# Exp groups of two PSUM banks with a third shared bank up to group 600, 101 VectorE quads, and the reciprocal multiply on GpSimd, in a fused attention and gated MLP block

## Chip, cores and metric

The kernel runs on one core of a Trainium2 chip. The metric is the device time in microseconds (us) of one execution. A core has five engines that work side by side: TensorE (PE in the profile, PEld for its weight loads), VectorE (DVE), ScalarE (ACT), GpSimd (POOL) and SyncE (SP), which here issues nearly all DMA transfers. TensorE writes its results into PSUM, eight banks of 128 partitions x 512 fp32 values; the other operands lie in SBUF.

## What is computed

The input x has 2048 rows of 640 values. The reference is a transformer block with modulation (adaLN), all weights in bf16:

```python
mod = (_silu(c) @ w_mod).reshape(c.shape[0], 6, 1, -1)   # sa, ca, ga, sb, cb, gb
h = _layernorm(x) * (1 + ca) + sa
x = x + ga * A(h)      # attention: 32 heads of 20, softmax(q k^T / sqrt(20)) v, then @ wo
h = _layernorm(x) * (1 + cb) + sb
x = x + gb * B(h)      # B(h) = ((h @ w_gate) * (h @ w_up)) @ w_down, inner width 1536
```

The 32 x 2048 x 2048 softmax exponentials are the large elementwise part.

## The kernel before

**Tiling.** The queries are cut into five chunks of 512, 512, 512, 256 and 256 rows (CHUNKS, L400). The heads are taken four at a time, in 8 sets; a chunk with a set of heads is an item, so there are 40 items. Within an item the work is cut into units: one head, one PSUM bank of scores (128 keys x 512 queries, or 2 x 128 keys x 256 queries). An item of a 512-row chunk has 64 units, one of a 256-row chunk has 32. Scores stand with keys on the partitions. Score matmuls (L1204) use 32 rows of TensorE each, so four heads run side by side; the matmuls with V (L1666) use 32 columns each, so again four run side by side, all into PSUM bank 7.

**Two ways to an exponential.** Most units go to ScalarE: one ACTIVATE (L1238) takes a group of neighbouring score banks and writes bf16 probabilities into a ring (PPs, L547, 4 slots for each of two sets). The groups alternate between bank set A, which starts at bank 0, and set B, which starts at bank 3. Up to group HEADG (60, L404) every group has two banks; from then on set A has three banks (0, 1, 2) and set B two (3, 4); L1078 decides it. The other units go to VectorE, in quads of four units; QUADS (L401) says how many quads an item has. For a unit VectorE evacuates the scores as integers (L1262); for a quad it then makes a mantissa part (L1290), a product (L1295) and an exponent part (L1298), which stand for the exponential as a sum of two terms. Both terms are multiplied with V, so such a unit costs two V matmuls in place of one. D_LEAD sets how early within the sequence a quad's scores are due.

**PSUM.** Five banks belong to the exp groups and bank 7 to the V accumulation. The rest is the pool G (L619), from which everything else takes its bank: projections of Q, K and V, the output projection, the MLP, the VectorE quads' scores and filler matmuls. G starts with banks 5, 6 and 2. Bank 2 leaves it when group HEADG is near (HEAD_OUT groups ahead, L1817) and then serves as the third bank of set A.

**After an item.** When all V matmuls of an item are done, VectorE transposes the accumulator (L1343), takes the reciprocal of the softmax sums (L1346), multiplies (L1348) and transposes back (L1355); DMAs put the result in place for the output projection. With T3_POOL (L407) the multiply goes to GpSimd instead, on all items but the last (L1351).

**What sets the order.** A planner in the program (class Sched, L114) plays all tasks through at build time with costs of its own and writes a fixed instruction order for each engine, with semaphore waits. TensorE's turn is chosen in pick_pe (L1814): a score group first if its banks are free, with up to two units of VectorE quads attached to it; then V matmuls, then the other work by priority and gate (the number of exp groups started), then filler matmuls where TensorE's recent activity is low. Until STEAL_END (L25) ScalarE may take over PSUM evacuations from VectorE when it has nothing to do (steal, L240). After chunk c its output projection, second layernorm and MLP (suffix, L1388) run spread over the exps of chunk c + 1, by GATE_F; after the last chunk they form the tail. The K projections of a key tile in K_ALL go directly into place (kq_round, L878); those of the others are computed packed, five rounds of up to 128 columns, written to DRAM and read back in the layout that the scores need (packed_round, L929).

```python
1078        us = ubuf[ap:ap + (3 if even and len(glist) >= HEADG else 2)]
...
1817        if HEADG and g >= HEADG - HEAD_OUT and 2 not in G.gone:
1818            G.retire(2)
```

Of the kernel before, what the change touches and what calls it, by code (L numbers as in the profile page):

```python
# [6 lines left out]
ALU = mybir.AluOpType  # L7
# [14 lines left out]
T0 = 700.0  # L22
DMA_SLOW = 0.0015
DMA_LAT = 1700.0
STEAL_END = 94936.728  # L25
STEAL_GAP = 300.0
HAM_W = 3413.3
HAM_MIN = 2550.0
# [369 lines left out]


CHUNKS = [(0, 512), (512, 512), (1024, 512), (1536, 256), (1792, 256)]  # L400
QUADS = [(3, 3, 3, 3, 3, 3, 4, 3), 3, (3, 3, 3, 3, 3, 3, 4, 3), (1, 2, 1, 2, 1, 2, 0, 2), 1]  # L401
D_LEAD = 0.35
NB0, NSS = 2, 3
HEADG = 60  # L404
GU_ONE = 0
XCONT = 0
T3_POOL = 0  # L407
HEAD_OUT = 1
NPS = 4
TS_4X, TT_2X = 600.0, 1145.0  # L410
WM_GATE = 18
WM_NEED = 1.721
K_DIRECT = (0, 1, 2, 3)
Q_DIRECT = 2
K_LEAD = 0.567
K_ALL = (0, 1)
KD_LEAD = 0.559
DMA_WINDOW = 900000
D_LATE = 12
D_RES = 92  # L420
PVMIN, PVMAX, PVCAP = 2, 11, 18
GATE_F = [0.8, 0.893, 0.938, 0.5, 1.0]
FILL_MIN = 4200.0
DUP_MIN = 0.0
XN_POOL = ()
XFIRST = 0
LN2P = 1.495
NALT = 1
OPFIRST = 0
HT_L = 0.072  # L430
V_L = 0
LATE_A = 1.174
LATE_L = 2.164
LATEQ = (3,)
LATEQ_A = 7
LATEQ_F = 0.73
QUAD_GAIN = 0.597233983857778
NTERM = 2

# [9 lines left out]
def build_kernel(nc, A_x, A_wqkv, A_wo, B_x, B_w_gate, B_w_up, B_w_down, c, w_mod, out):  # L449
# [5 lines left out]
    NSET = 8  # L455
# [141 lines left out]

    set_r = (hprod, h2T, xck, xn2)
    ntail = CHUNKS[-2][1]
    q_dead = sum(NSET * n * 2 for (_, n) in CHUNKS[:-1])  # L600
    set_t = None
    t_size = 0
    if NALT:
        T = Sub(qt_off, sum(NSET * n * 2 for (_, n) in CHUNKS[:2]))
        set_t = (T.alloc("hprodt", [128, FT, ntail], BF16), T.alloc("h2Tt", [128, KD, ntail], BF16),
                 T.alloc("xckt", [128, ntail // 128, D], BF16), T.alloc("xn2t", [128, ntail // 128, D], BF16))
        t_size = T.off - qt_off
# [661 lines left out]
    for qi, (it, us) in enumerate(dquads):  # L1269
        st_ = d_state[qi]  # L1270
        st_["src"], st_["ss"] = {}, {}

        def term(f, deps, dur, name, slot=None, src=None, last=False, it=it, qi=qi, st_=st_):
            t = Task("dve", dur, f, deps, prio=2.5 + .001 * qi, name=f"{name}.{qi}")
            if slot is not None:
                t.acq = [(sSS, "s", 1)]
            t.cond = lambda: it <= st_pv["item"]

            def on_t(task):
                if slot is not None:  # L1280
# [12 lines left out]
        def fx(e, st_=st_):  # L1293
            d = DSS[:, st_["ss"][0], :].bitcast(BF16)
            return e.tensor_tensor(d, DB0[:, st_["slot"], :].bitcast(BF16), d, ALU.mult)  # L1295

        def fe(e, st_=st_):
            return e.tensor_scalar(DSS[:, st_["ss"][1], :], DB0[:, st_["slot"], :], 0x7F80, 2, op0=ALU.bitwise_and,  # L1298
                                   op1=ALU.bitwise_or)
        tm = term(fm, list(st_["p1"]), TS_4X, "M", slot=0)  # L1300
        term(fx, [tm], TT_2X, "X", src=0, last=True)
        term(fe, list(st_["p1"]), TS_4X, "EX", slot=1, src=1, last=True)

    first_pv = {}
# [276 lines left out]
    for it in range(len(items)):  # L1581
        ci, j = items[it]
        t1s[it] = item_end_tasks(it)
        if j == NSET - 1:
            sfx_done["qd1"] = [score_q[g][0] for g in range(NG) if any(u.ci == 1 for u in score_q[g][1])][-1:] + x0_done
            sfx_done["qdead"] = [score_q[g][0] for g in range(NG) if any(u.ci == NC - 2 for u in score_q[g][1])][-1:]
            suffix(ci)
    pvstate = {"sidx": 0, "didx": 0}
# [147 lines left out]
        g = pvstate["sidx"]  # L1736
        return g < NG and dst["next"] < len(dlist) and due[dst["next"]] + D_RES < apos[g]

    def pick_x(t):
        rl = sc.readyl["pe"]  # L1740
        rl.sort(key=lambda x: (x.prio, x.seq))
        cand = None
        if xcur[0] is not None:
            cand = xcur[0]
        else:
            for task in rl:
                if task.gate > sc.progress:
                    continue
                cand = task
                if task.acq and d_wants() and len(G.free) < 2:  # L1750
                    cand = None
# [62 lines left out]
    def pick_pe(t):  # L1814
# [4 lines left out]
        if g < NG:  # L1819
# [4 lines left out]
            if (g != HEADG or not HEADG or back[0]) and acquire_ready(ts, t):  # L1824
                start = mode_start("S", t)
                rows = {}
                for u in us:
                    rows[u.s] = rows.get(u.s, 0) + 1
                d_attach(ts, t, apos[g], rows, 2, False)
                dur = 216.0 * max(rows.values()) * clk()  # L1830
                area = 128.0 * sum(rows.values())
                if sc.recent(t) + area < DUP_MIN and sc.free_at["act"] > start + 2 * dur + 100:
# [26 lines left out]
        elif not tail_added[0]:  # L1859
# [5 lines left out]
                        G.add(b, la)  # L1865
            else:
                tail_added[0] = False
        if sc.recent(t) < FILL_MIN and ring() >= RINGLOW and pick_x(t):
            return True
        if XFIRST and ring() >= XFIRST and pick_x(t):  # L1870
            just_s[0] = False
# [21 lines left out]
            pv_issue(cands, t)  # L1893
            return True
        if t > 4000 and fill_ok(t, fill_deps):
            start = mode_start("X", t)
            fs = G
            if pvstate["sidx"] == 0:
                fs = next((q for q in (GX, GC) if q.avail() is not None and q.avail()[0] <= t), GC)
            task = Task("pe", 216.0, ffill, fill_deps, ctr="pex", mode="X", name="fill", acq=[(fs, "g", 1)])  # L1900
            if not sc.acquire(task, t):
                return False
            b_ = task.slots["g"]
            task.emits = [lambda e: e.matmul(
                ps[:, b_, :].rearrange("p (a b) -> p a b", a=4), ident[:], ident[:].unsqueeze(1).to_broadcast([128, 4, 128]))]
            sc.activity(start, 512.0)
            sc.left += 1
            sc.finish_issue(task, start, 216.0 * clk())
            fs.done(b_, task)
            sc.pe_mode = "X"  # L1910
            sc.pe_end = start + 216.0 * clk()
            sc.free_at["pe"] = sc.pe_end
            sc.nfill += 1
            return True
        return False

    fill_deps = [p_id]
    ffill = None
# [58 lines left out]
```

The softmax here doesn't subtract the row's maximum and nothing guards it: scores larger than these inputs give would overflow.

## Time and profile before

| what | value |
|---|---|
| median of 5 runs | 843.82 us (839.83 to 845.13) |
| the profiled execution | 840.94 us |
| its span, first to last instruction | 839.1 us |
| exps on ACT (L1238) | 683 |
| VectorE quads | 93 (L1295 x93, L1262 x372) |
| mean granted TensorE clock | 0.99 |
| last exp ends | 804.4 us into the span |

The profile is of one execution, so its durations are summed against its own 840.94 us and not against the median. "L1238" is line 1238 of the kernel. In a row on a group of instructions the number after x is the count; behind the bar stand the busy time in us, the mean duration in ns and, after the next bar, the idle time of the engine before them with what ended it. A stage row gives a stretch of the span, its length, and for each engine the busy time with the count of instructions. A timeline row gives start and duration of a run of like instructions without a gap; where shapes alternate, it shows that of the first. Busy time counts a matmul from its start to its modelled end, so TensorE shown as busy isn't TensorE at its peak.

### The profile page before, as it was taken

How to read it: one execution, taken by the hardware profiler on the slowest of the kernel's cores; microseconds unless marked ns; L12 is line 12 of the kernel's file. 1: busy time of each engine (PE TensorE's matmuls, PEld its weight loads, DVE VectorE, ACT ScalarE, POOL GpSimd, SP SyncE). 2: the span in 40 equal slices, each digit the busy share in tenths (PEclk: the TensorE clock that was granted, in tenths of full speed). 3: DMA queues.
4: the chain of work that ended last, by engine and by line, in shares of the span. 5: the costliest groups of instructions: out<-in, count | busy, mean ns of one | idle time of the engine just before them, and what ended most of it. 6: DMA issues, size and time to landing. Idle time of an engine off the chain costs nothing.

```text
span 839.1 us, 28098 instructions
## 1 busy us (share of the span) xinstructions
PE 791.4 (94%) x12268; PEld 305.6 (36%) x12268; DVE 714.3 (85%) x1266; ACT 782.6 (93%) x719; POOL 31.7 (4%) x65
## 2 busy tenths in 40 slices
PE   8999989999999999999999999999999999999998
PEld 4433333222233222223333222233244433454477
DVE  7988989888899988898799988889779969677773
ACT  4789999998999999999999999999999999999931
POOL 2300000000001000000001000000000000000000
PEclk9999999998999999999999999999999999999999
DMA  9244210112240222310400222000400236124520
GB/s 302 60 139 118 70 43 18 29 45 86 70 117 20 46 52 64 107 44 22 100 2 5 53 48 46 16 11 13 99 4 5 62 77 135 38 58 88 122 60 20
DMA packets 113889, 52.77 MB, mean 63 GB/s; under 512 B 83231, under 2 KB 113767, under 8 KB 113767
## 3 DMA queue, kind: packets, MB, share of 16 engines
q1 hardware_dynamic: 112839, 49.83, 23.4%
q8 instruction: 97, 1.59, 0.8%
q10 hardware_dynamic: 928, 1.15, 0.4%
q14 instruction: 25, 0.20, 0.1%
HBM read 40.83 MB, written 7.82 MB: 58 GB/s over the span
## 4 chain that ended last, share of the span: by engine, by line
PE 48%; ACT 24%; DVE 18%; issue 8%; DMA 1%; POOL 0%; ACTq 0%; DVEq 0%
ACT PP L1238 24%; PE ps_all L768 17%; PE ps_all L1204 15%; PE ps_all L1666 10%; DVE DB L1262 6%; PE ps_all L935 3%; DVE DSS L1295 2%; PE ps_all L883 2%; DVE DSS L1290 1%; DVE DSS L1298 1%; DVE OT L1343 1%; DMA wm<-in_w_mod_dram 1%; PE ps_all L850 1%; DVE xck L1432 1%; DVE st L1442 1%
## 5 line engine op out<-in xcount | busy, mean ns | idle before, releaser
L1238 ACT ACTIVATE PP<-ps_all 128x1024 bf16<-128x1024 f32 (+2 forms) x683 | 763.6, 1300 | 8.1 <-PE ps_all L1204 7.3
L1204 PE MATMUL ps_all<-QT,KT 32*128 32x512 bf16 (+1 forms) x2560 | 308.9, 341 | 26.7 <-ACT PP L1238 21.8
L1262 DVE TENSOR_SCALAR DB<-ps_all 128x512 int16<-128x512 f32 x372 | 251.3, 684 | 63.6 <-PE ps_all L1204 61.8
L1204 PEld LDWEIGHTS ps_all<-QT,KT 32*128 32x128 bf16 x2560 | 82.6, 91 | 261.9 <-ACT PP L1238 190.1
L1666 PE MATMUL ps_all<-PP,Vf 128*32 128x512 bf16 (+2 forms) x2112 | 165.2, 343 | 0.0
L768 PE MATMUL ps_all<-h2T,stg 128*32 128x512 bf16 x1440 | 111.2, 382 | 4.9 <-DVE DB L1262 3.4
L1295 DVE TENSOR_TENSOR DSS<-DB,DSS 128x2048 bf16<-128x2048 bf16 x93 | 112.9, 1214 | 0.1
L1666 PEld LDWEIGHTS ps_all<-PP,Vf 128*32 128x32 bf16 (+1 forms) x2112 | 47.8, 94 | 87.2 <-issue 79.3
L1666 PE MATMUL ps_all<-DSS,Vf 128*32 128x512 bf16 (+3 forms) x896 | 73.7, 347 | 0.0
L1290 DVE TENSOR_SCALAR DSS<-DB 128x2048 int16<-128x2048 int16 x93 | 63.4, 682 | 1.4
L1298 DVE TENSOR_SCALAR DSS<-DB 128x2048 int16<-128x2048 int16 x93 | 63.6, 684 | 0.2 <-PE ps_all L1666 0.2
L768 PE MATMUL ps_all<-wd,hprod 128*32 128x320 bf16 x1152 | 57.1, 301 | 1.4 <-DVE DB L1262 0.7
L768 PEld LDWEIGHTS ps_all<-h2T,stg 128*32 128x32 bf16 x1440 | 33.7, 95 | 41.8 <-issue 14.5
L1343 DVE STREAM_TRANSPOSE OT<-ps_all 128x512 f32<-128x512 f32 (+1 forms) x40 | 24.2, 606 | 13.4 <-PE ps_all L1666 13.3
L768 PEld LDWEIGHTS ps_all<-wd,hprod 128*32 128x32 bf16 x1152 | 27.7, 96 | 20.5 <-issue 8.8
L768 PE MATMUL ps_all<-wo,Ocp 128*32 128x320 bf16 x640 | 33.3, 301 | 0.6 <-DVE xck L1432 0.2
L1535 DVE CAST gsb<-ps_all 128x512 bf16<-128x512 f32 (+1 forms) x48 | 29.5, 614 | 3.4 <-PE ps_all L768 3.2
L1445 POOL TENSOR_SCALAR sd<-mv 128x1 f32<-128x1 f32 x14 | 5.8, 416 | 696.4 <-DVE mv L1444 696.4
L768 PE MATMUL ps_all<-wV,hT 128*32 128x320 bf16 x640 | 31.1, 306 | 0.3 <-DVE DB L1262 0.2
L935 PE MATMUL ps_all<-hT,wq 128*32 128x512 bf16 x375 | 30.0, 400 | 0.8 <-DVE DB L1262 0.8
L1666 PEld LDWEIGHTS ps_all<-DSS,Vf 128*32 128x32 bf16 (+1 forms) x896 | 22.9, 95 | 20.2 <-issue 10.7
L1546 DVE TENSOR_TENSOR hprod<-ps_all,gsb 128x512 bf16<-128x512 f32 x36 | 24.6, 684 | 4.4 <-PE ps_all L768 4.1
(108 smaller groups left out, 526.9 us busy)
## 6 DMA issues: line engine op xcount, KB each, us to landing
stg<-in_B_w_gate_dram SPq DMA_DIRECT2D x50, 160.0 KB
stg<-in_B_w_up_dram SPq DMA_DIRECT2D x50, 160.0 KB
QT<-q_rows SPq DMA_DIRECT2D x22, 128.0 KB
wm<-in_w_mod_dram SPq DMA_DIRECT2D x3, 800.0 KB
x<-in_A_x_dram SPq DMA_DIRECT2D x7, 320.0 KB
xck<-in_A_x_dram SPq DMA_DIRECT2D x3, 640.0 KB
wd<-in_B_w_down_dram SPq DMA_DIRECT2D x1, 1920.0 KB
out_dram<-xck SPq DMA_DIRECT2D x12, 160.0 KB
```

Source lines behind the costliest of these rows:

```text
L768: return lambda e, b: e.matmul(ps[32 * x:32 * x + 32, b, c0:c0 + n], lhs()[:, 32 * x:32 * x + 32], rhs(), tile_position=(0, 32 * x), start ...
L935: f = [lambda e, b_, k=k, x=x: e.matmul(ps[x:x + min(32, w - x), b_, :], wx[:, k, r0 + x:r0 + min(x + 32, w)], hT[tc][:, k, :], tile_posit ...
L1204: ems.append(lambda e, i=i, kt=kt: e.matmul(dstf()[:, i * u.n:(i + 1) * u.n], KT[32 * u.s:32 * u.s + 32, u.j, kt * 128:(kt + 1) * 128], QT ...
L1238: return e.activation(PPs[g % 2][:, cellp["p"], 0:nu * 512], ps[:, b0:b0 + nu, :].rearrange("p b c -> p (b c)"), AFT.Exp, scale=ESCALE)
L1262: return e.tensor_scalar(DB0[:, st_["slot"], x * 512:(x + 1) * 512], bank(cell["b"]), EBIAS, 0.0, op0=ALU.add, op1=ALU.max)
L1290: return e.tensor_scalar(DSS[:, st_["ss"][0], :], DB0[:, st_["slot"], :], 0x7F, 0x3F00, op0=ALU.bitwise_and, op1=ALU.bitwise_or)
L1295: return e.tensor_tensor(d, DB0[:, st_["slot"], :].bitcast(BF16), d, ALU.mult)
L1298: return e.tensor_scalar(DSS[:, st_["ss"][1], :], DB0[:, st_["slot"], :], 0x7F80, 2, op0=ALU.bitwise_and, op1=ALU.bitwise_or)
L1343: t1 = Task("dve", n * 1.1 + 70, lambda e: e.transpose(OT[:, 0:n], ps[:, BPV, 0:n]), [], prio=0.0, name=f"T1.{it}")
L1535: f = lambda e: e.tensor_copy(gsb[:, gs, 0:n], ps[:, r.b["b"], 0:n])
L1546: f = lambda e: e.tensor_tensor(hprod[:, fc, 0:n], ps[:, r.b["b"], 0:n], gsb[:, gs, 0:n], ALU.mult)
L1666: ems.append(lambda e, i=i, kt=kt, stt=stt, stp=stp: e.matmul(ps[32 * s:32 * s + mc, BPV, 0:u.n], Vf[:, (kt * H + 4 * u.j + s) * VW:(kt * ...
```

## The change

Constants of the planner change, three of them with weight: HEADG goes from 60 to 600, so that exp groups have two banks and bank 2 stays in the shared pool up to group 600; QUADS goes from 93 to 101 quads; T3_POOL is set, which puts the reciprocal multiply of 39 of the 40 items on GpSimd. K_ALL loses key tile 1. The other numbers are gates, leads and due times. The code gains options: a GpSimd form of the quad's product (X_POOL, 0), early attaching of quads (EAGER, 0), a hard floor and another matmul form for filler (FILL_HARD 0.0, FILL_MODE 'X'), and a rule that the matmuls named "col" (the modulation vectors) are not taken as filler after STEAL_END. NQT evaluates to 1, the index that stood there before. Diff, with hunks that only thread these options through left out:

```diff
@@ -22,7 +22,7 @@
 T0 = 700.0
 DMA_SLOW = 0.0015
 DMA_LAT = 1700.0
-STEAL_END = 94936.728
+STEAL_END = 85877.564
 STEAL_GAP = 300.0
 HAM_W = 3413.3
 HAM_MIN = 2550.0
@@ -398,42 +398,46 @@
 
 
 CHUNKS = [(0, 512), (512, 512), (1024, 512), (1536, 256), (1792, 256)]
-QUADS = [(3, 3, 3, 3, 3, 3, 4, 3), 3, (3, 3, 3, 3, 3, 3, 4, 3), (1, 2, 1, 2, 1, 2, 0, 2), 1]
-D_LEAD = 0.35
+QUADS = [(2, 3, 3, 3, 4, 3, 4, 3), (3, 4, 3, 4, 3, 4, 3, 4), (3, 4, 3, 4, 3, 4, 3, 4), (1, 2, 1, 2, 1, 2, 1, 2), 1]
+D_LEAD = 0.384
 NB0, NSS = 2, 3
-HEADG = 60
+HEADG = 600
+EAGER = 0
+X_POOL, X_PIECES, POOL_NS = 0, 4, 2.2
 GU_ONE = 0
 XCONT = 0
-T3_POOL = 0
-HEAD_OUT = 1
+T3_POOL = 1
+HEAD_OUT = 2
 NPS = 4
 TS_4X, TT_2X = 600.0, 1145.0
-WM_GATE = 18
-WM_NEED = 1.721
+WM_GATE = 15
+WM_NEED = 1.824
 K_DIRECT = (0, 1, 2, 3)
 Q_DIRECT = 2
-K_LEAD = 0.567
-K_ALL = (0, 1)
-KD_LEAD = 0.559
+K_LEAD = 0.703
+K_ALL = (0,)
+KD_LEAD = 0.686
 DMA_WINDOW = 900000
-D_LATE = 12
-D_RES = 92
-PVMIN, PVMAX, PVCAP = 2, 11, 18
-GATE_F = [0.8, 0.893, 0.938, 0.5, 1.0]
+D_LATE = 13
+D_RES = 75
+PVMIN, PVMAX, PVCAP = 2, 13, 16
+GATE_F = [0.8, 0.788, 1.0, 0.673, 1.0]
 FILL_MIN = 4200.0
+FILL_HARD = 0.0
+FILL_MODE = 'X'
 DUP_MIN = 0.0
 XN_POOL = ()
 XFIRST = 0
 LN2P = 1.495
 NALT = 1
 OPFIRST = 0
-HT_L = 0.072
-V_L = 0
-LATE_A = 1.174
-LATE_L = 2.164
+HT_L = 0.099
+V_L = 0.079
+LATE_A = 1.127
+LATE_L = 3
 LATEQ = (3,)
-LATEQ_A = 7
-LATEQ_F = 0.73
+LATEQ_A = 0
+LATEQ_F = 0.561
 QUAD_GAIN = 0.597233983857778
 NTERM = 2
...
@@ -597,11 +601,12 @@
 
     set_r = (hprod, h2T, xck, xn2)
     ntail = CHUNKS[-2][1]
+    NQT = next(i for i in range(NC) if CHUNKS[i][0] + CHUNKS[i][1] >= 1024)
     q_dead = sum(NSET * n * 2 for (_, n) in CHUNKS[:-1])
     set_t = None
     t_size = 0
     if NALT:
-        T = Sub(qt_off, sum(NSET * n * 2 for (_, n) in CHUNKS[:2]))
+        T = Sub(qt_off, sum(NSET * n * 2 for (_, n) in CHUNKS[:NQT + 1]))
         set_t = (T.alloc("hprodt", [128, FT, ntail], BF16), T.alloc("h2Tt", [128, KD, ntail], BF16),
                  T.alloc("xckt", [128, ntail // 128, D], BF16), T.alloc("xn2t", [128, ntail // 128, D], BF16))
...
@@ -1298,7 +1303,25 @@
             return e.tensor_scalar(DSS[:, st_["ss"][1], :], DB0[:, st_["slot"], :], 0x7F80, 2, op0=ALU.bitwise_and,
                                    op1=ALU.bitwise_or)
         tm = term(fm, list(st_["p1"]), TS_4X, "M", slot=0)
-        term(fx, [tm], TT_2X, "X", src=0, last=True)
+        if X_POOL and qi % X_POOL == 0:
+            deps = [tm]
+            for x in range(X_PIECES):
+                w = 2048 // X_PIECES
+
+                def fxp(e, x=x, w=w, st_=st_):
+                    d = DSS[:, st_["ss"][0], x * w:x * w + w].bitcast(BF16)
+                    return e.tensor_tensor(d, DB0[:, st_["slot"], x * w:x * w + w].bitcast(BF16), d, ALU.mult)
+                t = Task("pool", w * POOL_NS + 150.0, fxp, deps, prio=.1 * qi, name=f"XP.{qi}")
+
+                def on_p(task, x=x, st_=st_):
+                    if x == X_PIECES - 1:
+                        sB0.done(st_["slot"], task)
+                        st_["src"][0] = [task]
+                t.on_start = on_p
+                sc.add(t)
+                deps = [t]
+        else:
+            term(fx, [tm], TT_2X, "X", src=0, last=True)
         term(fe, list(st_["p1"]), TS_4X, "EX", slot=1, src=1, last=True)
 
...
@@ -1744,7 +1767,7 @@
             cand = xcur[0]
         else:
             for task in rl:
-                if task.gate > sc.progress:
+                if task.gate > sc.progress or (warm and task.name[:3] == "col" and t > STEAL_END):
                     continue
                 cand = task
...
@@ -1865,7 +1888,9 @@
                         G.add(b, la)
             else:
                 tail_added[0] = False
-        if sc.recent(t) < FILL_MIN and ring() >= RINGLOW and pick_x(t):
+        if sc.recent(t) < FILL_MIN and ring() >= RINGLOW and pick_x(t, True):
+            return True
+        if sc.recent(t) < FILL_HARD and t > 20000 and do_fill(t):
             return True
         if XFIRST and ring() >= XFIRST and pick_x(t):
             just_s[0] = False
@@ -1893,26 +1918,35 @@
             pv_issue(cands, t)
             return True
         if t > 4000 and fill_ok(t, fill_deps):
-            start = mode_start("X", t)
-            fs = G
-            if pvstate["sidx"] == 0:
-                fs = next((q for q in (GX, GC) if q.avail() is not None and q.avail()[0] <= t), GC)
-            task = Task("pe", 216.0, ffill, fill_deps, ctr="pex", mode="X", name="fill", acq=[(fs, "g", 1)])
-            if not sc.acquire(task, t):
-                return False
-            b_ = task.slots["g"]
-            task.emits = [lambda e: e.matmul(
-                ps[:, b_, :].rearrange("p (a b) -> p a b", a=4), ident[:], ident[:].unsqueeze(1).to_broadcast([128, 4, 128]))]
-            sc.activity(start, 512.0)
-            sc.left += 1
-            sc.finish_issue(task, start, 216.0 * clk())
-            fs.done(b_, task)
-            sc.pe_mode = "X"
-            sc.pe_end = start + 216.0 * clk()
-            sc.free_at["pe"] = sc.pe_end
-            sc.nfill += 1
-            return True
+            return do_fill(t)
         return False
+
+    def do_fill(t):
+        mode = FILL_MODE if pvstate["sidx"] else "X"
+        start = mode_start(mode, t)
+        fs = G
+        if pvstate["sidx"] == 0:
+            fs = next((q for q in (GX, GC) if q.avail() is not None and q.avail()[0] <= t), GC)
+        task = Task("pe", 216.0, ffill, fill_deps, ctr="pex", mode=mode, name="fill", acq=[(fs, "g", 1)])
+        if not sc.acquire(task, t):
+            return False
+        b_ = task.slots["g"]
+        idb = ident[:].unsqueeze(1).to_broadcast([128, 4, 128])
+        if mode == "X":
+            task.emits = [lambda e: e.matmul(ps[:, b_, :].rearrange("p (a b) -> p a b", a=4), ident[:], idb)]
+        else:
+            task.emits = [lambda e, x=x: e.matmul(
+                ps[32 * x:32 * x + 32, b_, :].rearrange("p (a b) -> p a b", a=4), ident[:, 32 * x:32 * x + 32], idb,
+                tile_position=(0, 32 * x), skip_group_check=True) for x in range(4)]
+        sc.activity(start, 512.0)
+        sc.left += 1
+        sc.finish_issue(task, start, 216.0 * clk())
+        fs.done(b_, task)
+        sc.pe_mode = mode
+        sc.pe_end = start + 216.0 * clk()
+        sc.free_at["pe"] = sc.pe_end
+        sc.nfill += 1
+        return True
 
     fill_deps = [p_id]
     ffill = None
```

More of the change, by code (lines that the diff above doesn't have):

```diff
@@ L1584, in build_kernel @@
         if j == NSET - 1:
-            sfx_done["qd1"] = [score_q[g][0] for g in range(NG) if any(u.ci == 1 for u in score_q[g][1])][-1:] + x0_done
+            sfx_done["qd1"] = [score_q[g][0] for g in range(NG) if any(u.ci == NQT for u in score_q[g][1])][-1:] + x0_done
             sfx_done["qdead"] = [score_q[g][0] for g in range(NG) if any(u.ci == NC - 2 for u in score_q[g][1])][-1:]
@@ L1737, in d_wants, with pick_x @@
         return g < NG and dst["next"] < len(dlist) and due[dst["next"]] + D_RES < apos[g]
-    def pick_x(t):
+    def pick_x(t, warm=False):
         rl = sc.readyl["pe"]
@@ L1828, in pick_pe @@
                     rows[u.s] = rows.get(u.s, 0) + 1
-                d_attach(ts, t, apos[g], rows, 2, False)
+                d_attach(ts, t, apos[g] + EAGER, rows, 2, False)
                 dur = 216.0 * max(rows.values()) * clk()
```

## The prediction, made before the change was run

> **What bounds the kernel now.** I read the page's busy shares first, then the busy times by stage, then the timeline of the exp engine, then who waits for whom, and last the costs of single instructions.
>
> ```profile
> PE 791.4 (94%) x12268; PEld 305.6 (36%) x12268; DVE 714.3 (85%) x1266; ACT 782.6 (93%) x719; POOL 31.7 (4%) x65
> ```
>
> The averages name two candidates, PE and ACT. I cut the span where the exps of a query chunk begin, by counting exps along ACT's timeline (units per chunk below): chunk 0 from 17 us (92 us is its exp group 60), chunk 1 from 228.6, chunk 2 from 416.7, chunk 3 from 603.7, chunk 4 from 700.9 to 804.4. Busy time by stage:
>
> ```profile
> 17.00:92.00 75.00, 73.84 (x1101) 30.10 (x1101) 67.40 (x138) 64.96 (x76) 10.07 (x23) 0.95 0.40 111
> 92.00:228.60 136.60, 128.32 (x1615) 39.63 (x1607) 121.25 (x191) 133.36 (x119) 0.00 (x0) 0.98 0.19 51
> 228.60:416.70 188.10, 178.62 (x2340) 58.14 (x2339) 171.11 (x282) 188.08 (x168) 5.07 (x8) 1.00 0.24 62
> 416.70:603.70 187.00, 175.70 (x2215) 56.08 (x2215) 166.59 (x268) 186.98 (x166) 5.44 (x8) 1.00 0.13 32
> 603.70:700.90 97.20, 92.58 (x1668) 39.30 (x1666) 81.94 (x151) 96.79 (x86) 4.04 (x8) 1.00 0.18 44
> ```
>
> Columns: PE, weight load, VectorE, ACT, GpSimd, clock, DMA. From 206 us to 804 us ACT never rests: the kernel is bound by exp there. VectorE has 17.0 us left in chunk 1 and 20.4 us in chunk 2. Behind the last exp stand 34.7 us of tail.
>
> PE looks nearly as full, but in chunk 1 its weight loads wait most for ACT to give exp banks back:
>
> ```profile
> PEld ps_all L1204 <- ACT PP L1238: 53.8, 138, 0.9
> PEld ps_all L1666 <- issue: 23.5, 93, 0.4
> ```
>
> A wait of 0.23 us stands before nearly every change of matmul kind ("issue" too), so of 53.8 us about 53.8 - 138 x 0.23 = 22 us is real slack.
>
> ACT's timeline gives the price of one exp better than its duration, since neighbours overlap:
>
> ```profile
> 17.34 5.61 ACT L1238 ACTIVATE PP<-ps_all 128x1024 bf16<-128x1024 f32 x6
> 77.03 15.94 ACT L1238 ACTIVATE PP<-ps_all 128x1024 bf16<-128x1024 f32 x17 [0.28 <-PE ps_all L1204]
> 206.16 430.39 ACT L1238 ACTIVATE PP<-ps_all 128x1536 bf16<-128x1536 f32 x380 [1.55 <-PE ps_all L1204]
> ```
>
> ```profile
> L1238 ACT ACTIVATE PP<-ps_all 128x1536 bf16<-128x1536 f32 x311 | 478.0, 1537 | 2.8 <-PE ps_all L1204 2.2 <-PE ps_all L1666 0.2
> L1238 ACT ACTIVATE PP<-ps_all 128x1024 bf16<-128x1024 f32 x371 | 403.7, 1103 | 5.3 <-PE ps_all L1204 5.1
> L1262 DVE TENSOR_SCALAR DB<-ps_all 128x512 int16<-128x512 f32 x372 | 251.3, 684 | 63.6 <-PE ps_all L1204 61.8
> L1295 DVE TENSOR_TENSOR DSS<-DB,DSS 128x2048 bf16<-128x2048 bf16 x93 | 112.9, 1214 | 0.1
> L1348 DVE TENSOR_TENSOR OTn<-OT,invT 128x512 bf16<-128x512 f32 x24 | 16.4, 684 | 0.1
> ```
>
> A two-bank exp repeats every (5.61 - 1.10) / 5 = 0.90 us; a third bank adds 1.537 - 1.103 = 0.434. So a bank (a unit) costs 0.434 us and an instruction 0.90 - 0.868 = 0.034 us on top.
>
> **The change part by part.**
>
> Exp work moved. There are 3 x 8 x 64 + 2 x 8 x 32 = 2048 units. 93 quads leave 1676 to ACT (412, 416, 412, 212, 224 by chunk), 101 leave 1644 (412, 400, 400, 208, 224). 32 units less: -32 x 0.434 = -13.9 us.
>
> More, smaller exps. Before: 60 groups of two banks, then 1556 units by pairs of 3 + 2, 623 groups: 683. After: 600 groups hold 1200 units, just short of the end of chunk 2 (1212); 444 units make 178 more: 778. 95 more instructions x 0.034 = +3.2 us. Here a rule speaks against the change: the Trainium skill ("ScalarE: Activation LUTs", What ACT_TABLE_LOAD costs) gives an ACTIVATE 186 ns plus its elements, 280 ns with a pointer operand, and back-to-back ones overlap by 93 ns. By it each extra exp costs 93 to 187 ns, 8.8 to 17.8 us, and the upper end would eat all that the quads save. The repeat of 0.90 us decides: 1024 elements at the page's 0.833 ns leave about 0.05. I take 0.034; at 0.05 it would be 4.8.
>
> Refilling every set in 0.90 us. Two-bank sets must be refilled while ACT works off two banks, each time; now every second refill has 1.33 us. The loss today: 430.39 / 380 = 1.133 us an exp, clean would be (0.90 + 1.334) / 2 = 1.117, so 0.016. The nearest row for two-bank groups with a shared third bank is the stretch of 17: (15.94 - 1.10) / 16 = 0.928, a loss of 0.028; but PE was 98% busy there, 95% in chunks 1 and 2. Upper bound: 540 groups x 0.028 + 178 x 0.016 - 623 x 0.016 = +8 us. Lower bound: at 0.00 as in the stretch of 6, -7 us. I take +3. PE itself pays some 95 extra score blocks of about 0.45 us (0.22 stream, two changes of kind of about 0.1): 34 x 0.45 = 15 us in chunk 1, hidden in the 22 us of slack, which are nearly used up; uncovered it would be ACT's loss.
>
> Eight more quads on VectorE. A quad is four L1262, one L1290, L1295 and L1298. In VectorE's timeline two L1262 back to back take 1.28 us, so one repeats at 0.60; the quad is 4 x 0.60 + 0.60 + 1.13 + 0.60 = 4.73 us. Chunk 1 gets four (+18.9), chunk 2 three (+14.2), chunk 3 one; chunk 0 keeps 25. Each unit is also multiplied with V twice on PE, 32 matmuls more, 4 side by side: 32 / 4 x 0.22 = 1.8 us, hidden.
>
> Reciprocal multiply to GpSimd. It takes 24 x 0.60 + 15 x 0.34 = 19.5 us off VectorE (the last item stays), 4.8 in each of chunks 1 and 2. No row shows such a GpSimd instruction; the Trainium skill ("GPSIMD Engine Reference", 3.1) has 4497 ns for 2048 elements, an estimate of 1.1 to 1.3 us for 512. Against it stands "SBUF — State Buffer", Who interferes with whom: GpSimd and VectorE hold a shared port pair exclusively when VectorE runs a two-port mode or has two SBUF inputs, as L1290, L1298 and L1295 do. The trace bears on it from one side, GpSimd's:
>
> ```profile
> 250.82 0.22 POOL L1445 TENSOR_SCALAR sd<-mv 128x1 f32<-128x1 f32 x1 [2.75 <-DVE mv L1444]
> 251.13 1.52 POOL L1447 TENSOR_TENSOR rs<-sd,mhalf 128x1 f32<-128x1 f32 x1
> 260.42 1.19 POOL L1445 TENSOR_SCALAR sd<-mv 128x1 f32<-128x1 f32 x1 [2.14 <-DVE mv L1444]
> 261.68 0.57 POOL L1447 TENSOR_TENSOR rs<-sd,mhalf 128x1 f32<-128x1 f32 x1
> ```
>
> The same one-column instructions take 0.22 or 1.19, 0.57 or 1.52 us: about 1 us more, an L1295 long. So the multiply will take 1.2 to 2.3 us. The transpose L1355 waits for it, and L1262 evacuations queue behind that wait; score banks and PE wait for those. Bounds for VectorE: -19.5 us (nothing blocked), or 39 x 1.2 = 47 us blocked, +27. Without the lock the sum is the first, with the lock in every case the second. Half an item's 0.6 us lost each time is my choice: about 0.3 + 0.3 us of blocking and waiting cancel the saving.
>
> So VectorE in chunk 1: 171.1 + 18.9 - 4.8 = 185 us unblocked, for about 188.1 - 16 x 0.434 + 34 x 0.034 = 182 us of ACT; in chunk 2: 166.6 + 14.2 - 4.8 = 176 for 183. Together 361 of 365, and 371 if the saving is lost. The exp outputs have 8 slots, some 8 us of play, and a third shared bank shortens VectorE's 13.8 us of waits for scores in chunk 1. I charge +2 us.
>
> Edits at nothing: one K tile goes through DRAM as five packed rounds in place of seven direct ones (PE -2 rounds of about 1.1 us, VectorE -1.2 us; 34 more DMAs on SP, where two take 0.82 us to issue, past the weight and Q loads; cover: the lead of 0.703 items, about 18 us; gone, a late K row stops all score groups). Gates, due times, the earlier end of ACT's help: these reorder work in a start where ACT works on exps 55.6 of 75 us; bounds -4 to +4, taken as 0. The new options (eager, GpSimd X term, hard fill) are off; the rule on column tasks moves only filler.
>
> Sum: -13.9 + 3.2 + 3 + 2 = -5.7 us. The profiled execution took 840.94 (span 839.1 and 1.84 around it), giving 835.2; it lies 2.9 under the median of 843.82, so in the runs' terms 838.1.
>
> **The rivals.**
> - Bigger gain, 831: refills cost nothing more (-3), VectorE copes (-2), the half-clock episode before 206 us, where ACT waits 2.5 us, doesn't recur (-2.5): -13.2 in all. For it: the clean 0.90. Against: 98% PE in the only two-bank stage. Chance 0.14.
> - VectorE becomes the bound in chunks 1 and 2, 843: 371 us of work plus 1% of idleness is 375, what both chunks take today; chunk 3 returns 1.7 and chunk 0 adds 1.0, -0.7 in all; with 2% of idleness it is +3. For it: 98% load before any blocking. Against: it idles mostly for lack of scores. Chance 0.25.
> - Slower, 852: score refill in a two-bank rhythm fails. A refill queues behind a block of V matmuls (up to 0.6 us in PE's timeline) and two changes of kind. If the loss per two-bank exp reaches 0.06 us, 540 x 0.06 - 7 = +25, minus 10.7 is +14 at the far end, and +8 at 0.048. It decides from 0.041 us, where +4.2 is passed. For it: PE's slack of 22 us less 15. Against: ACT's two-bank stretches today lose 0.028 at most with full clock. Chance 0.23.
> - The likeliest, ACT still the bound with part of the gain, 834 to 840: 0.38.
>
> **How the numbers follow.** 0.5% (4.2 us) is about what a measurement of this kernel can tell from no change. Faster: 0.38 and 0.14, less the 0.02 above 839.6: 0.50. Same: 0.25 and 0.02, 0.27. Slower: 0.23. Range 827 to 854: it leaves out the far ends of both outer cases, some 0.04 below and 0.09 above; the likeliest's own is 834 to 840.
>
> **What would show it.** Right: 778 exps, ACT above 99% in chunks 1 and 2, two-bank stretches at or under 0.92 us, VectorE about 97% there. The multiply on GpSimd at 1.2 us with stretched ones near 2.3, and L1295 or L1298 lengthened where they meet it. Wrong: ACT idle behind scores in chunks 1 or 2 (PE), or L1355 waiting for GpSimd for more than 10 us in all (VectorE). An exp repeat over 0.95 us would make the prediction wrong altogether.

## The result and the profile after

| what | before | changed |
|---|---|---|
| median | 842.82 us (80 runs, 838.62 to 845.79) | 839.64 us (43 runs, 837.1 to 848.86) |
| span of the profiled execution | 839.1 us | 837.6 us |
| exps on ACT | 683 | 778 |
| filler matmuls | 60 | 119 |

The ratio is 0.9969 with an interval of 0.9959 to 0.9978: 0.31% faster. That is clear of the measurement over so many runs, but under the 0.5% that the prediction set as its bound. The change moves 32 units away from the engine that set the pace and rebuilds its rhythm, and 3 us come of it. So the question is where the gain went.

The granted clock qualifies these 3 us. In some stretches, of 3.4 us or a multiple, the profile shows half the full clock granted to TensorE; they lower the mean clock of an execution. Among the executions for which it is on record, the median of the mean clock is 0.988 before and 0.996 changed, and within each kernel a lower clock goes with a longer time. At 0.994 to 0.996 both kernels cover the same times: 838.9 to 839.7 us before (4 executions), 837.6 to 843.3 us changed (27). So no gain is shown between executions at the same clock. The gain of the medians goes with fewer stretches at half clock, and no run separates these from the order of the work that may cause them.

The page's busy shares of the changed kernel:

```profile
PE 809.3 (97%) x12313; PEld 305.5 (36%) x12313; DVE 732.3 (87%) x1286; ACT 780.8 (93%) x809; POOL 78.4 (9%) x104
```

TensorE went from 94% to 97%; ACT stands where it was. In the page's chain of work that ended last, TensorE's share rose from 48% to 64% and ACT's fell from 24% to 12%. The stages, cut as before where the exps of a chunk begin (columns: PE, weight load, VectorE, ACT, GpSimd, clock, DMA):

```profile
18.00:86.70 68.70, 67.48 (x1039) 27.29 (x1039) 62.15 (x128) 63.27 (x73) 14.00 (x25) 1.00 0.42 123
86.70:223.25 136.55, 135.03 (x1700) 40.47 (x1696) 126.98 (x204) 136.35 (x147) 8.12 (x5) 1.00 0.29 76
223.25:412.50 189.25, 185.23 (x2324) 56.99 (x2319) 181.85 (x297) 187.62 (x201) 16.27 (x16) 1.00 0.20 52
412.50:599.70 187.20, 182.50 (x2257) 56.91 (x2253) 175.11 (x279) 186.04 (x199) 19.06 (x16) 1.00 0.14 33
599.70:697.30 97.60, 93.19 (x1650) 39.68 (x1646) 83.07 (x148) 96.15 (x86) 9.57 (x16) 0.98 0.15 34
```

Set against the stages of before, from the starts of the exps in both traces:

| stretch | before, us | changed, us | difference |
|---|---|---|---|
| start to first exp | 17.3 | 18.5 | +1.1 |
| first exp to group 60 | 76.7 | 68.2 | -8.5 |
| rest of chunk 0 | 134.5 | 136.6 | +2.0 |
| chunk 1 (416, now 400 units) | 189.4 | 189.3 | -0.1 |
| chunk 2 (412, now 400 units) | 186.6 | 187.2 | +0.6 |
| chunk 3 (212, now 208 units) | 96.3 | 97.6 | +1.3 |
| chunk 4 | 102.9 | 101.9 | -0.9 |
| after the last exp | 34.8 | 37.8 | +3.0 |

(The last exp's own 0.6 us stands in no row.) From group 60 to the last exp, where the 32 units were to pay, nothing is gained: +2.9 us. In this pair of traces, whose spans differ by 1.5 us, all of the gain is in the first 87 us, which the prediction left at zero. Two cautions belong to the 8.5 us. The trace of before has two half-clock stretches of 3.4 us there (at 44 and 72 us), the changed one none before 677 us. And group 60 isn't quite the same point of the work, since the first item leaves 52 units to ACT before and 56 now; up to the start of chunk 1, after 412 units in both, the gain from the first exp on is 6.5 us (211.3 to 204.8).

ACT's timeline of the changed kernel shows what the exps cost now. Its columns are start, duration, and the count of exps without a recorded gap:

```profile
80.08 152.61 ACT L1243 ACTIVATE PP<-ps_all 128x1024 bf16<-128x1024 f32 x163 [0.31 <-PE ps_all L1209]
261.00 96.00 ACT L1243 ACTIVATE PP<-ps_all 128x1024 bf16<-128x1024 f32 x100 [0.35 <-PE ps_all L1209]
357.34 89.37 ACT L1243 ACTIVATE PP<-ps_all 128x1024 bf16<-128x1024 f32 x97 [0.34 <-PE ps_all L1209]
```

From the start of the first to the start of the last exp of a row, one repeats at 0.935, 0.959 and 0.919 us. Counted by start to start, the 550 two-bank exps between units 100 and 1200 average 0.942, with a shortest steady step of 0.904. A unit costs 0.471 us in this rhythm; in the pairs of 3 and 2 banks of before it cost 2.265 / 5 = 0.453 (chunks 1 and 2). That answers for chunks 1 and 2 to within 2 us (1.7 worked out, 0.5 measured): 28 units less are worth 28 x 0.453 = 12.7 us, and the other 800 now cost 800 x 0.018 = 14.4 us more.

The waits in chunk 1 of the changed kernel, TensorE's weight loads, then VectorE, and last VectorE in chunk 1 of before:

```profile
PEld ps_all L1209 <- ACT PP L1243: 49.7, 132, 0.8
PEld ps_all L1689 <- issue: 23.7, 101, 0.4
```

```profile
DVE DB L1267 <- PE ps_all L1209: 3.3, 4, 1.9
```

```profile
DVE DB L1262 <- PE ps_all L1204: 13.8, 19, 1.6
```

By the reading of the prediction TensorE's slack is 49.7 - 132 x 0.23 = 19 us, little less than before (22). VectorE's wait for scores fell from 13.8 to 3.3 us, which is what the third shared bank was put there for: VectorE is busy for 181.9 of 189.3 us (before 171.1 of 188.1).

The multiply on GpSimd and one of VectorE's masks, groups of the changed kernel:

```profile
L1371 POOL TENSOR_TENSOR OTn<-OT,invT 128x512 bf16<-128x512 f32 x24 | 38.0, 1585 | 472.9 <-DVE invT L1369 472.9
L1303 DVE TENSOR_SCALAR DSS<-DB 128x2048 int16<-128x2048 int16 x101 | 72.3, 716 | 0.0
```

A mask took 684 ns on average and at most 696 before; now it takes 716 on average and up to 1542. One such meeting, GpSimd first, then VectorE, each from its timeline:

```profile
277.60 1.37 POOL L1371 TENSOR_TENSOR OTn<-OT,invT 128x512 bf16<-128x512 f32 x1 [21.91 <-DVE invT L1369]
```

```profile
277.97 1.54 DVE L1303 TENSOR_SCALAR DSS<-DB 128x2048 int16<-128x2048 int16 x1
```

The mask starts while the multiply runs and ends 0.54 us after the multiply's end at 278.97. So VectorE stood still behind GpSimd, as the Trainium skill ("SBUF — State Buffer", Who interferes with whom) has it. It came cheap: the two masks L1303 and L1295 grew by 0.032 and 0.008 us on average, 101 of each, some 4 us in all, and 3.6 us of VectorE waiting for the multiply's result, against 19.5 us of work taken off.

### The profile page after: what moved, and what is told of

Its sections match the earlier page's. It is cut to its first block, busy times and chain, and to the rows that moved or that the text cites. A ratio compares the mean times of both kernels' runs of the same rounds, so it can differ in the third digit from the quotient of the medians.

```text
span 837.6 us, 28503 instructions
## 1 busy us (share of the span) xinstructions
PE 809.3 (97%) x12313; PEld 305.5 (36%) x12313; DVE 732.3 (87%) x1286; ACT 780.8 (93%) x809; POOL 78.4 (9%) x104
## 4 chain that ended last, share of the span: by engine, by line
PE 64%; DVE 18%; ACT 12%; issue 5%; POOL 1%; DVEq 0%; ACTq 0%
PE ps_all L773 22%; PE ps_all L1209 20%; PE ps_all L1689 14%; ACT PP L1243 12%; DVE DB L1267 6%; PE ps_all L940 4%; DVE DSS L1300 2%; DVE DSS L1303 2%; DVE st L828 1%; PE ps_all L888 1%; DVE DSS L1295 1%; DVE OT L1366 1%; PE ps_all L1936 1%; DVE OcT L1378 1%; POOL OTn L1371 1%
## 5 line engine op out<-in xcount | busy, mean ns | idle before, releaser
L1243 ACT ACTIVATE PP<-ps_all 128x1024 bf16<-128x1024 f32 (+1 forms) x778 | 765.0, 1102 | 6.2 <-PE ps_all L1209 4.2
L1209 PE MATMUL ps_all<-QT,KT 32*128 32x512 bf16 (+1 forms) x2560 | 319.5, 340 | 12.4 <-ACT PP L1243 7.6
L1267 DVE TENSOR_SCALAR DB<-ps_all 128x512 int16<-128x512 f32 x404 | 267.9, 683 | 42.4 <-PE ps_all L1209 40.8
L1689 PE MATMUL ps_all<-PP,Vf 128*32 128x512 bf16 (+3 forms) x2076 | 161.4, 343 | 0.4 <-DVE OT L1366 0.4
L1300 DVE TENSOR_TENSOR DSS<-DB,DSS 128x2048 bf16<-128x2048 bf16 x101 | 122.4, 1212 | 0.0
L1371 POOL TENSOR_TENSOR OTn<-OT,invT 128x512 bf16<-128x512 f32 (+1 forms) x39 | 48.0, 1230 | 612.4 <-DVE invT L1369 612.4
L1689 PE MATMUL ps_all<-DSS,Vf 128*32 128x512 bf16 (+1 forms) x968 | 79.8, 350 | 1.1 <-DVE DSS L1300 0.5
L1303 DVE TENSOR_SCALAR DSS<-DB 128x2048 int16<-128x2048 int16 x101 | 72.3, 716 | 0.0
L1295 DVE TENSOR_SCALAR DSS<-DB 128x2048 int16<-128x2048 int16 x101 | 69.7, 690 | 0.9
L1936 PE MATMUL ps_all<-ident 128*128 128x512 bf16 x119 | 43.6, 417 | 1.9 <-POOL ident L729 1.5
L1689 PEld LDWEIGHTS ps_all<-DSS,Vf 128*32 128x32 bf16 x968 | 24.5, 95 | 27.5 <-issue 12.0
```

The source lines that it names most:

```text
L1209: ems.append(lambda e, i=i, kt=kt: e.matmul(dstf()[:, i * u.n:(i + 1) * u.n], KT[32 * u.s:32 * u.s + 32, u.j, kt * 128:(kt + 1) * 128], QT ...
L1243: return e.activation(PPs[g % 2][:, cellp["p"], 0:nu * 512], ps[:, b0:b0 + nu, :].rearrange("p b c -> p (b c)"), AFT.Exp, scale=ESCALE)
L1267: return e.tensor_scalar(DB0[:, st_["slot"], x * 512:(x + 1) * 512], bank(cell["b"]), EBIAS, 0.0, op0=ALU.add, op1=ALU.max)
L1371: f3 = lambda e: e.tensor_tensor(OTn[:, 0:n].rearrange("p (b c) -> p b c", c=32), OT[:, 0:n].rearrange("p (b c) -> p b c", c=32), invT[:, ...
L1689: ems.append(lambda e, i=i, kt=kt, stt=stt, stp=stp: e.matmul(ps[32 * s:32 * s + mc, BPV, 0:u.n], Vf[:, (kt * H + 4 * u.j + s) * VW:(kt * ...
L1936: task.emits = [lambda e: e.matmul(ps[:, b_, :].rearrange("p (a b) -> p a b", a=4), ident[:], idb)]
```

## The experiments

Two theories stood at the start. **V**: VectorE, now 96% busy in chunk 1, paces the exps. **P**: TensorE paces them, since it has to refill two banks every 0.9 us. Exps are timed from start to start in the traces, and the mean of these steps is called the repeat. "Full clock" leaves out the half-clock stretches, 5 us ahead of each and 8 us behind it.

**VectorE made light.** Same order of instructions on every engine.

```diff
-  e.tensor_scalar(DB0[:, slot, x*512:(x+1)*512], bank(b), ...)
+  e.tensor_scalar(DB0[:, slot, x*512:x*512 + lw//4], bank(b)[:, 0:lw//4], ...)   # lw = 512 from quad 6 on
   # mantissa, product and exponent parts likewise on 0:lw of 2048 columns
```

> The changed kernel with every engine's instructions in the same order, but from the seventh quad on VectorE's quad instructions (evacuation, mantissa, product, exponent) work on a quarter of their columns; the output is left incomplete by that. A quad costs about 1.5 us of VectorE instead of 4.73. Theory V (VectorE, 96% busy in chunks 1 and 2, paces them): the repeat of a two-bank exp falls from 0.942 to about 0.91 us and chunks 1 and 2 take 182 to 184 us each instead of 189.3 and 187.2; the total falls by 8 to 12 us. Theory P (TensorE, 98% busy there, paces them by refilling two banks every 0.9 us): the repeat stays within 0.935 to 0.945, both chunks stay within 1.5 us, the total within 3 us of the changed kernel.

One execution took 830.61 us, span 828.7, at the mean clock of the changed kernel's trace (0.998). Its chunks 1 and 2:

```profile
222.10:408.70 186.60, 184.17 (x2324) 56.52 (x2323) 101.91 (x297) 186.35 (x201) 12.07 (x16) 1.00 0.20 53
408.70:593.70 185.00, 181.61 (x2257) 55.86 (x2253) 94.90 (x278) 184.83 (x200) 12.26 (x16) 1.00 0.14 33
```

VectorE drops to 55% and the chunks lose 2.7 and 2.2 us, the repeat goes from 0.942 to 0.933. Neither theory's number: VectorE makes a quarter of the loss over 0.904, and the other three quarters stay with VectorE half idle. The span's 8.9 us come from all stages: 2.7 + 2.2 + 2.1 (chunk 3, where the changed kernel has its half-clock stretch and this one has none) + 0.7 (chunk 4), 1.1 before the first exp.

**V matmuls halved**, in the changed kernel and in the one before.

```diff
-                ps[32 * s:32 * s + mc, BPV, 0:u.n],
+                ps[32 * s:32 * s + mc, BPV, 0:u.n // 2],
-                srcf()[:, i * u.n:(i + 1) * u.n], ...
+                srcf()[:, i * u.n:i * u.n + u.n // 2], ...
 # the accumulator bank is also preset to 1.0 in place of 0.0
```

> The changed kernel with the same order on every engine, but each matmul with V streams half of its columns; the output is left incomplete by that. It takes about 17 us of streaming from TensorE in each of chunks 1 and 2 and nothing from VectorE or ACT. Theory P: the exp repeat falls from 0.942 to at most 0.92 us, chunks 1 and 2 lose 4 us or more each. Theory V: the repeat and both chunks stay as they are (within 1.5 us). If the lighter TensorE is throttled to half clock in places, only the unthrottled stretches count.

> The same halved V matmuls in the kernel before, where exps of 3 and 2 banks alternate; the output is left incomplete. A pair of exps repeats at 2.285 us there against 2.235 clean. Theory P gives TensorE a smaller part in the kernel before: chunks 1 and 2 shorten by 1 to 3 us each, less than half of what the changed kernel gains from the same cut. If TensorE holds both kernels back alike, the gain is equal in both.

They took 860.55 and 847.58 us, one execution each, longer than with full matmuls. During the exps of the first, TensorE was given half clock for 102 us (3.4 us in the changed kernel), in stretches of up to 37.5 us: less work brought the slower clock, so the totals tell nothing of refills. Full-clock stretches do. Chunk 0 of the changed kernel ran from 87.3 us without throttling:

```profile
87.30:221.30 134.00, 127.69 (x1700) 40.86 (x1692) 126.38 (x204) 133.87 (x148) 8.14 (x5) 1.00 0.30 77
```

134.0 us against 136.6, VectorE as busy as with full matmuls. The repeat is 0.918 there (0.936 with full matmuls); at full clock in chunks 1 and 2 it is 0.921 and 0.928, where the same exps of the changed kernel take 0.935 and 0.940. Over all 505 two-bank exps from group 60 on that ran at full clock in both, 0.939 falls to 0.923, and the steps that are over 0.1 us late fall from 77 to 25. In the kernel before, a pair went from 2.266 to 2.256 in chunk 1, 0.005 an exp (the expectation's 2.285 is about the average from group 60 to the last exp, 2.282). So TensorE's work does lengthen the repeat, by some 0.016 us of the 0.038 lost, and less so in the old rhythm. That is P, with a size: the larger of the two, but not the whole. Chunks 1 and 2 as wholes stay unmeasured for the throttling.

**The multiply back on VectorE.**

```diff
-T3_POOL = 1
+T3_POOL = 0
```

> The changed kernel with the reciprocal multiply back on VectorE. In the changed kernel's trace 39 multiplies took 48 us of GpSimd, the longest mantissa and exponent instructions of VectorE grew from 0.70 to 1.54 us, some 4 us of blocking in all, and VectorE waited 3.6 us for GpSimd, against 19.5 us of instructions saved. Theory V: chunks 1 and 2 lengthen by 3 to 5 us each and the total by 6 to 10. Theory P: within 2 us in chunks 1 and 2; the rest is order.

842.66 us, ratio to before 1.0013 (0.9988 to 1.0038), so about 3.7 us over the changed kernel's 0.9969 x 842.82. Chunk 1 takes 2.2 us more, chunk 2 1.1 less, the rest of chunk 0 the same; the head (+1.5, with a half-clock stretch at 75 us) and the tail (+1.6) hold most. Between the two expectations again. The planner orders the work anew here, so the 3.7 us are those of the move with its order; what VectorE alone gives isn't separated. At the same clock some 2 us are left: at 0.998 or above this kernel has a median of 841.3 us (5 executions) and the changed one of 839.5 (10). For all its blocking the move to GpSimd is worth keeping.

**The quads of before.**

```diff
-QUADS = [(2,3,3,3,4,3,4,3), (3,4,...), (3,4,...), (1,2,1,2,1,2,1,2), 1]
+QUADS = [(3,3,3,3,3,3,4,3), 3, (3,3,3,3,3,3,4,3), (1,2,1,2,1,2,0,2), 1]
```

> The changed kernel with the 93 quads of before (25, 24, 25, 11, 8), all else as changed, so two-bank groups up to group 600 with less work on VectorE. Theory R (a unit costs 0.47 us in two-bank groups that are refilled every 0.9 us, against 0.453 in pairs of 3 and 2): chunks 1 and 2, of 416 and 412 units, take 208 x 0.935 = 194 and 193 us, and the total is 10 to 15 us above the changed kernel's 839.6. Theory V (VectorE paces): with VectorE back at 90% the repeat falls to 0.91 and the chunks take 189 and 187, the total within 3 us.

858.51 us, ratio 1.0195 (1.017 to 1.022). Chunks 1 and 2:

```profile
229.40:426.70 197.30, 191.95 (x2351) 59.23 (x2344) 166.38 (x271) 195.41 (x210) 18.14 (x16) 1.00 0.19 50
426.70:618.70 192.00, 185.71 (x2262) 57.20 (x2260) 162.03 (x257) 191.22 (x203) 18.35 (x16) 1.00 0.14 32
```

VectorE is at 84%, yet the repeat is 0.945 (0.942 at full clock). The rhythm costs what it costs, with or without the eight quads. Theory V is out as the main cause. The total lies 19 us above the changed kernel, more than the expected 10 to 15: group 60 comes 5.3 us later in the head (73.5 us in place of 68.2), and chunk 1 takes 3 us more than expected.

**Pairs of 3 and 2 banks with 101 quads.**

```diff
-HEADG = 600
+HEADG = 60
```

> The changed kernel with pairs of 3 and 2 banks from group 60 on, so with two shared banks for its 101 quads. If only the rhythm counts (theory R alone), chunks 1 and 2 of 400 units take 400 x 0.453 = 181 us each, 8 and 6 less than changed. If the third shared bank is what lets VectorE and TensorE carry 101 quads (theory B), VectorE waits longer for scores, chunks 1 and 2 take 188 us or more, or TensorE's other work is left over and the tail of 37.8 us grows by more than 5.

875.36 us, ratio 1.040 (1.034 to 1.047). Chunks 1 and 2 take 196.3 and 188.5 us, and the tail after the last exp 58.9. ACT's waits, then that of the changed kernel:

```profile
ACT gsb L1560 <- PE ps_all L773: 44.2, 12, 29.6
ACT PP L1243 <- PE ps_all L1209: 23.0, 28, 1.7
```

```profile
ACT PP L1243 <- PE ps_all L1209: 4.2, 10, 0.8
```

23.0 us of exps wait openly for scores (4.2 in the changed kernel), ten half-clock stretches lie between group 60 and the last exp, and projection work is left over for the end. These are the signs that were named for theory B, that 101 quads need the third shared bank. They don't prove it. At full clock a unit costs 0.467 and 0.459 us in chunks 1 and 2, more than the 0.453 of before but not more than the 0.471 of the changed kernel, so most of what these chunks lose goes with the half-clock stretches; and the gates and leads were set for the other rhythm. What the run shows is that the two parts can't be taken apart with these settings.

**The head alone, on the kernel before.**

```diff
-QUADS = [(3, 3, 3, 3, 3, 3, 4, 3), ...   K_ALL = (0, 1)   K_LEAD = 0.567   WM_GATE = 18   STEAL_END = 94936.728
+QUADS = [(2, 3, 3, 3, 4, 3, 4, 3), ...   K_ALL = (0,)     K_LEAD = 0.703   WM_GATE = 15   STEAL_END = 85877.564
 # also KD_LEAD, WM_NEED, HT_L, V_L, LATE_A, LATE_L of the changed kernel
```

> The kernel before with the head of the changed one: the first chunk's quads (2,3,3,3,4,3,4,3), one K tile direct, the leads and gates of the K, V and modulation work, the earlier end of ACT's help; pairs of 3 and 2 banks from group 60, 93 quads, the multiply on VectorE. If these settings made the changed kernel's head 8.5 us shorter (76.7 to 68.2 us from the first exp to group 60), it takes 68 to 71 us here, and the rest is like before: 836 to 842. If the head was longer in the profile of before by its two half-clock episodes at 44 and 72 us, which needn't recur, it takes 73 us or more.

848.46 us, ratio 1.0075 (1.004 to 1.011). The head and the rest of chunk 0:

```profile
17.30:86.05 68.75, 66.54 (x996) 26.00 (x988) 61.76 (x126) 62.86 (x73) 9.93 (x22) 0.98 0.44 124
86.05:228.05 142.00, 132.99 (x1690) 43.35 (x1682) 127.84 (x203) 132.69 (x118) 0.00 (x0) 0.99 0.22 60
```

68.7 us to group 60: these settings bring group 60 forward, without bank, rhythm or multiply, and although a half-clock stretch fell into it. But in this order the rest of chunk 0 gives 7.5 us back, chunks 1 and 2 another 3.0 and 3.9, with four half-clock stretches. Chunk 0 as a whole takes 210.7 us from its first exp, as good as before (211.3; changed 204.8). So the settings move the head's gain, but that they cause the kernel's gain isn't shown: alone they make it slower. Of the eleven settings one can be told apart. The run with the quads of before (quads93) has the other ten and all else of the changed kernel, and takes 73.5 us to group 60 and 210.6 for chunk 0, also with one half-clock stretch in its head. So some 5 of the 8.5 us go with where the 25 quads of chunk 0 stand, a part of it perhaps only because the first item then leaves ACT four units more.

**Fillers made light.** Same order.

```diff
-task.emits = [lambda e: e.matmul(ps[:, b_, :]..., ident[:], idb)]
+task.emits = [lambda e: e.matmul(ps[:, b_, 0:16], ident[:], ident[:, 0:16])]   # after the first 30 us
```

> The changed kernel with the same order, but filler matmuls after the first 30 us stream 16 columns in place of 512. 119 fillers (60 before) keep TensorE's clock up. If fillers take time that score refills need, the exp repeat falls below 0.935 us and the total by 2 us or more. If they stand where TensorE would idle, and the clock needs them, half-clock stretches come up and the total rises by 3 us or more.

887.44 us. The page's row of the granted clock, in 40 slices of the span:

```profile
PEclk9999999995695699979876699999569999999999
```

The mean is 0.898 instead of 0.998, with stretches at half clock of up to 41 us. At full clock the repeat stays at 0.938 to 0.947, and exp by exp it equals that of the changed kernel (0.938 in both over 111 exps of chunk 1, 0.946 over 113 of chunk 2). So the 119 fillers take nothing from the refills, and with them cut to 16 columns this one execution took nearly 50 us longer.

**Shorter V blocks.**

```diff
-PVMIN, PVMAX, PVCAP = 2, 13, 16
+PVMIN, PVMAX, PVCAP = 2, 13, 8
```

> The changed kernel with at most 8 units in one block of V matmuls in place of 16 (a planner limit, so some order changes with it). If a refill is late because it queues behind a long block of V matmuls, the repeat of a two-bank exp falls below 0.935 us in chunks 1 and 2. If it is late by the fixed costs of changing between score, V and other matmuls, the repeat stays at 0.94 to 0.95 or rises, since shorter blocks mean more changes, and the total stays or rises by up to 5 us.

844.35 us, ratio 1.002 (1.0003 to 1.0038); repeat at full clock 0.944 and 0.949. Long V blocks aren't what makes refills late; with shorter ones it is a little worse. That fits fixed costs of changing the kind of matmul, but doesn't show them by themselves.

**Other settings in the same form.**

```diff
 retuned_a: HEADG 580, 100 quads, WM_GATE 1, GATE_F (0.886, 0.851, 0.868, 0.766), PVMAX 10, PVCAP 19
 retuned_b: HEADG 560, 101 quads, WM_GATE 0, GATE_F (0.623, 0.935, 0.814, 0.729), PVMAX 14, PVCAP 19
```

> The changed kernel with other gates, leads and limits (two-bank groups to 580, 100 quads, the modulation loads not gated, suffix gates 0.886, 0.851, 0.868, 0.766, V blocks of up to 19). By the runs so far the body can't gain much (0.94 us a two-bank exp in every form with fillers), so what is left is the head (68.2 us) and the tail (37.8). I expect 834 to 840 us: up to 3 us from a shorter tail and head, lost again if half-clock stretches fall into the exps.

> As the other retuned kernel with a second set: two-bank groups to 560, 101 quads, suffix gates 0.623, 0.935, 0.814, 0.729. I expect 834 to 841 us for the same reasons.

836.57 us, ratio 0.9936 (0.9914 to 0.9957), and 837.7, ratio 0.9941 (0.9919 to 0.9963): both beat the kernel before. Against the changed kernel (0.9959 to 0.9978) the first is just clear, the second overlaps. The first has a repeat of 0.943 as well; it gains 1.1 us to the first exp, 1.1 in the head, 0.4 and 0.6 in chunks 1 and 2, loses 1.2 in the rest of chunk 0, and its tail is 35.0 us instead of 37.8. The second needs 72.9 us to group 60, 4.7 more than the changed kernel, and is no slower: the short head isn't needed for the gain. At a clock of 0.992 it took 837.4 to 837.9 us (5 executions), where before took 839.9 to 840.3 (5) and the changed kernel 840.8 to 841.7 (3).

## Why the prediction was right and wrong, point by point

The time (838.1, measured 839.64) lay close, inside the 834 to 840 of the likeliest case. That is luck: two large errors had opposite signs, and the base of 843.82 came down to 842.82 with more runs. The gain was about half of the 0.68% forecast (0.31% by the ratio, 0.38% by the medians). By the prediction's own line of 0.5% it is no change, to which it had given 0.27, and not the "faster" of 0.50. The repeat of 0.942, with 0.959 in one stretch, lay between the 0.92 that was to show it right and the 0.95 that was to show it wrong.

- **Units and exps.** Clean steps in the traces are 0.904 and 1.331 us, so a bank costs 0.427 and an exp 0.050 on top: 32 x 0.427 = 13.7 off, 95 x 0.050 = 4.8 on. The forecast had 13.9 and 3.2. The repeat of 0.90 us decided rightly against 93 to 187 ns an exp; 0.034 was too low because I took the bank from two mean durations.
- **Refilling every set: the step that failed.** "I take +3" where I had bounded it by +8. From group 60 to the last exp the clean steps make 695.1 us before and 686.2 changed; the traces show 709.7 and 712.5. The loss rose from 14.6 to 26.3 us: +11.7, against +3 for refills and +2 for VectorE. (Without the half-clock stretches it rose from 11.6 to 24.5.) Most of the 24.5 us are 104 two-bank steps that came over 0.1 us late; before there were 44. The nearest row, the two-bank stretch with its 0.928, would have given +8, and I set it aside since TensorE was busier there (98% against 95%). The changed kernel brings TensorE to 98% in chunks 1 and 2 itself. The slack of 22 us, of which the extra blocks were to take 15, still reads 19, so it was no measure of how late a refill comes. The case named as slower had the mechanism that the halved V matmuls bear out in part, at 0.038 us an exp, just under the 0.041 from which it was to decide.
- **VectorE.** Right that chunk 1 would run at 96 to 97% and that its waits for scores would go (13.8 to 3.3 us). With VectorE made light 7.8 of the 26.3 us go (704.7 us in place of 712.5). How much of that is new with the change isn't known, since the kernel before wasn't run with a light VectorE.
- **GpSimd.** The durations over 512 columns were 1.05 to 1.9 us (I had 1.2 to 2.3). The blocking came, but at 4 + 3.6 us in place of all 19.5. I set the whole saving to zero; the run with the multiply on VectorE puts it at about 3.7 us, the new order included.
- **The head.** "Taken as 0", bounds -4 to +4. It gave -8.5 to group 60 and -6.5 to the end of chunk 0, outside the bounds. ACT worked on exps for 55.6 of 75 us there; I named that idle time and didn't ask what other quads and gates would do with it, nor what two half-clock stretches in it cost.
- **The tail.** Not in the sum at all: +3.0. Of the MLP of chunk 3, TensorE has 60 matmuls left at the last exp instead of 12 (changed kernel, then before):

```profile
L773 PE MATMUL ps_all<-h2Tt,stg 128*32 128x256 bf16 x60 | 1.8, 272 | 0.0
```

```profile
L768 PE MATMUL ps_all<-h2Tt,stg 128*32 128x256 bf16 x12 | 0.5, 273 | 0.0
```

That makes 1.3 us by these rows. Whether TensorE's fuller body or the later gate of that MLP (GATE_F for chunk 3 went from 0.5 to 0.673) left them to the end, and what makes the rest, wasn't separated.

What stays open: how the late refills divide between TensorE's changes of kind and its stream; the third of the 0.038 us that, if the two add up, is left beside the lighter VectorE (0.009) and the halved V matmuls (0.016); and whether the gain of the medians is anything but the higher clock.

## What to carry to other kernels

An engine that shows 99% busy can still lose 4% in late steps that the busy share doesn't show: take the start-to-start repeat of its instructions and compare it with the shortest steady one, by shape. When work is cut into smaller pieces, cost the cover that each piece leaves to whoever refills it, from the nearest row of the same rhythm, and don't discount that row for being crowded when the change itself makes the place crowded. And put the stages that a change only reorders, the start above all, into the sum with bounds as wide as their idle time. Compare executions at the same granted clock before calling a difference of 0.3% a gain of the work.

## What the runs showed that I had not expected

- Taking work off TensorE slowed the kernel: halved V matmuls brought 102 us of half clock during the exps and 860.55 us, fillers cut to 16 columns 887.44 us at a mean clock of 0.898.
- A recorded exp grows longer when nothing holds it back: in a run of two-bank exps that start every 0.904 us (203 to 222 us of the changed kernel) the durations creep from 1.09 to 1.28 us, and fall to 1.02 after a late refill. The mean fell from 1103 to 1053 ns with the change, which looks like a gain but goes with more late refills.
- GpSimd's multiply over 512 columns took 1.05 us when no mask or product of VectorE ran at its start, 1.36 to 1.46 in the 8 cases where a mask did, and 1.90 to 1.91 in the 12 cases where the product L1300 did. In the other direction a mask that started inside the multiply took up to 1.54 us in place of 0.69.
